# A decode step of cached attention times a gated MLP on one core: the output weight's pieces are cut at block 15 instead of 18, and one piece is spread unevenly over the DMA engines

## The chip, the core and the metric

The kernel runs on one NeuronCore of one Trainium2 chip. The metric is device time in microseconds (us), the median of repeated runs. All arithmetic is in float32. The core has a matrix engine (PE, with its weight loads listed apart as PEld), a vector engine (DVE), a scalar engine (ACT), a general engine (POOL), and a synchronising engine (SP) whose queue issues nearly all the loads. The loads are carried out by 16 DMA engines that work side by side.

## The reference, cut to what matters

```python
xn = layernorm(x)                                 # 8 tokens x 512
q = (xn @ wq).reshape(B, 1, Hq, Dh)               # 32 heads of 128
k, v = repeat(k_cache, 4), repeat(v_cache, 4)     # 8 heads of 4096 x 128 for each token
p = softmax(q @ k.T * Dh ** -0.5)
s = (p @ v).reshape(B, 1, Hq * Dh) @ wo           # wo: 4096 x 512
g = silu(gmlp(xn))                                # w_in, gelu, layernorm, w_sp, w_out
out = x + s * g
```

The caches hold 268 MB, the three weights of the attention and the MLP the rest of the 290.8 MB that are read. Every byte is used once, with eight tokens to share it.

## The kernel before, in words

**Stages.** The MLP and the query projection come first, on weights loaded into two of three large SBUF slots (`slot_b`, `slot_c`; each 128 partitions by 64 KB). Then a loop runs over 16 units, each half the tokens of one key-value head: a unit's keys arrive in `slot_a`, its values in `slot_b`. PE computes scores into the PSUM bank `sc`, DVE and ACT do the softmax, PE transposes the probabilities and multiplies them with the values, and DVE keeps the diagonal blocks of the result in `o_sb`. At the start of the next turn PE's `combine(u)` (L311 to L316) folds `o_sb` into a column of `po`, and DVE copies it to `oT`.

**The output weight.** `wo` is 4096 x 512: 32 blocks of 128 rows, block m standing in the columns m*512 to (m+1)*512 of `slot_c`, so that one block is 2 KB in each of 128 partitions, 256 KB in all. It is loaded in seven pieces that `WO_PIECES` (L29) lists by their columns: blocks 0 to 17, 18 to 21, 22 to 25, 26 and 27, 28 and 29, 30 with the first half of 31, and the second half of 31. SP issues them one after the other (L416, L417) right behind the last unit's values, each over all 128 partitions and each with a semaphore of its own, and after them `x_res`, the residual (L418). The data of one DMA engine come in the order in which SP issued them.

**The projection.** For blocks 0 to 27 (`FOLDED`), whose heads are done before the last two units end, PE multiplies `oT` with the block into one of four quarters of `sc`, the quarter being the block's number modulo 4 (L438). Before the first block of a piece `need` (L423) makes PE wait for that piece's semaphore. At block 18 (`AHEAD`) PE runs `combine` for the last unit, which waits for DVE's tokens, and DVE makes `oT_last` of it. Blocks 28 and 29 then go, in eighths of 64 columns, directly into `acc` (L448); DVE copies `sc` to `o_all` when block 27 is done; PE adds it to `acc` with a selection matrix (`pick`, L460); blocks 30 and 31 follow (L448 again), the second half of 31 waiting for the last piece. DVE multiplies by the gate and adds the residual (L469, L470), and SP stores 32 KB (L472).

What sets the order around the change is thus the program's own text: SP's queue of loads, PE's sequence of blocks and the waits that `need` puts between them.

## Time and profile before

| what | value |
|---|---|
| device time, median of 3 runs (lowest, highest) | 678.82 us (678.7, 678.97) |
| the profiled execution: its own time, its span | 678.78 us, 677.3 us |
| PE busy, share of the span | 365.7 us, 54% |
| DVE busy, share of the span | 126.6 us, 19% |
| read from HBM, mean rate over the span | 290.77 MB, 429 GB/s |

The span runs from the first to the last event that the profile shows; 1.48 us of the execution lie around it. Where the stretches of the last microseconds are listed, "PEclk" is the share of TensorE's clock that was granted, and "DMA share" the mean busy share of the 16 DMA engines; a share of 0.25 is four engines' worth. In the list of DMA issues the last number is the time from issue to landing. A wait is shown in brackets at the instruction that followed it, with the one that ended it.

### The profile page before, as it was taken

What the parts mean: (1) busy time and instruction counts of PE and PEld (TensorE: products, weight loads), DVE (VectorE), ACT (ScalarE), POOL (GpSimd) and SP (SyncE); (2) the same over time, 40 slices, a digit from 0 to 9 for tenths busy, and PEclk for the clock granted to TensorE, in tenths of its full rate; (3) what the DMA queues carried; (4) which work ended last, traced back from release to release, by engine and by line L of the source; (5) the groups of instructions that cost most, each with busy time, mean ns of one, the idle gap of its engine ahead of it and who ended that gap; (6) DMA issues with size and microseconds to landing.
All of it is one profiled execution on the core that took longest, in us unless ns stands there. A gap on an engine that the chain in (4) does not pass through costs nothing. (4 is left out here: it accounts for less than half of the span.)

```text
span 677.3 us, 6222 instructions
## 1 busy us (share of the span) xinstructions
PE 365.7 (54%) x2524; PEld 121.7 (18%) x2524; DVE 126.6 (19%) x304; ACT 17.9 (3%) x51; POOL 3.7 (1%) x16
## 2 busy tenths in 40 slices
PE   0375645445665544465564445566554546656557
PEld 0121211111221111121121112122121212112122
DVE  2420201212120211212021121212021121202012
ACT  0000000000000000000000000000000000000000
POOL 1000000000000000000000000000000000000000
PEclk9796667788776667878766677887767788776569
DMA  9999999999999999999999999999999999999997
GB/s 388 433 434 434 434 433 433 433 433 433 433 433 433 433 433 433 433 433 433 433 433 433 433 433 433 433 433 433 433 433 433 433 433 433 437 433 433 445 433 300
DMA packets 6212, 290.86 MB, mean 429 GB/s; under 512 B 952, under 2 KB 1080, under 8 KB 1472
## 3 DMA queue, kind: packets, MB, share of 16 engines
q1 hardware_dynamic: 6192, 290.79, 99.3%
q8 instruction: 3, 0.05, 0.0%
q10 hardware_dynamic: 16, 0.02, 0.0%
q14 instruction: 1, 0.01, 0.0%
HBM read 290.77 MB, written 0.03 MB: 429 GB/s over the span
## 5 line engine op out<-in xcount | busy, mean ns | idle before, releaser
L294 PE MATMUL sc<-slot,qz 128*32 128x512 f32 x1024 | 147.0, 738 | 115.4 <-PEq L286 115.4
L304 PE MATMUL o_ps<-slot,pT 128*32 128x512 f32 x1024 | 146.0, 734 | 59.0 <-PEq L286 59.0
L294 PEld LDWEIGHTS sc<-slot,qz 128*32 128x32 f32 x1024 | 40.4, 132 | 208.9 <-issue 208.9
L304 PEld LDWEIGHTS o_ps<-slot,pT 128*32 128x32 f32 x1024 | 40.2, 132 | 156.7 <-issue 156.7
L342 DVE TENSOR_REDUCE nm<-sc 128x1 f32<-128x512 f32 x16 | 11.1, 691 | 278.4 <-DVEq L352 278.4
L342 DVE TENSOR_TENSOR o_all<-o_ps,diag 128x512 f32<-128x512 f32 x32 | 22.1, 691 | 165.0 <-DVEq L352 165.0
L342 DVE TENSOR_REDUCE o_sb<-o_all 128x128 f32<-128x512 f32 x32 | 33.5, 1046 | 1.1
L314 PE MATMUL po<-fold,o_sb 128*128 128x8 f32 x68 | 13.8, 277 | 32.2 <-PEq L283 32.2
L330 PE MATMUL t<-ident,p 128*128 128x128 f32 x64 | 17.2, 424 | 19.8 <-PEq L283 19.8
L402 ACT ACTIVATE p<-sc,nm 128x512 f32<-128x512 f32 x16 | 11.0, 687 | 576.7 <-ACTq L401 576.7
L314 PEld LDWEIGHTS po<-fold,o_sb 128*128 128x128 f32 x68 | 10.9, 202 | 47.2 <-issue 47.2
L327 PE MATMUL misc<-wl,peers 128*128 128x1 f32 x32 | 6.9, 284 | 19.1 <-PEq L283 19.1
L342 DVE COPY pT<-t 128x256 f32<-128x256 f32 x32 | 12.1, 419 | 22.8 <-DVEq L352 22.8
L330 PEld LDWEIGHTS t<-ident,p 128*128 128x128 f32 x64 | 11.2, 213 | 20.7 <-issue 20.7
L323 PE MATMUL misc<-ident,nm 128*1 128x128 f32 x16 | 4.3, 269 | 17.3 <-PEq L283 17.3
L325 PE MATMUL misc<-ident,row 1*128 1x1 f32 x16 | 3.0, 189 | 15.5 <-PEq L283 15.5
L207 PE MATMUL t<-slot,xnT 128*32 128x512 f32 (+1 forms) x32 | 5.5, 785 | 9.0 <-DMA slot<-in_w_mlp 9.0
L327 PEld LDWEIGHTS misc<-wl,peers 128*128 128x128 f32 x32 | 6.0, 234 | 20.0 <-issue 20.0
L438 PE MATMUL sc<-slot,oT 128*8 128x512 f32 x56 | 7.2, 593 | 2.1 <-DMA slot<-in_wo 2.1
L342 DVE TENSOR_SCALAR p<-p,w 128x512 f32<-128x512 f32 x16 | 7.8, 486 | 0.6
L268 PE MATMUL t<-slot,xnT 128*32 128x512 f32 x64 | 7.3, 594 | 0.0
L323 PEld LDWEIGHTS misc<-ident,nm 128*1 128x1 f32 x16 | 1.3, 79 | 31.3 <-issue 31.3
(81 smaller groups left out, 75.6 us busy)
## 6 DMA issues: line engine op xcount, KB each, us to landing
slot<-in_w_mlp SPq DMA_DIRECT2D x1, 5377.0 KB, 15.5
slot<-in_wo SPq DMA_DIRECT2D x1, 4608.0 KB, 39.5
slot<-in_wo SPq DMA_DIRECT2D x2, 1024.0 KB, 42.4
slot<-in_wo SPq DMA_DIRECT2D x2, 512.0 KB, 44.6
slot<-in_wo SPq DMA_DIRECT2D x1, 384.0 KB, 45.5
slot<-in_kT SPq DMA_DIRECT2D x16, 28.2
slot<-in_v SPq DMA_DIRECT2D x16, 29.1
slot<-in_wo SPq DMA_DIRECT2D x1, 128.0 KB, 45.3
```

What stands on the lines that cost most here:

```text
L207: i = te.matmul(pz[R * g:R * (g + 1), :, :n], xnT[:, k, :], w_in[:, k, :, lo:lo + n], start=(k == 0), stop=(k == NK - 1))
L268: i = te.matmul(t[0][R * g:R * (g + 1), :], xnT[:, k, :], wq_v[:, k, lo:lo + REP * DH], start=(k == 0), stop=(k == NK - 1))
L294: i = te.matmul(sc[R * g:R * (g + 1), :], qz[:, k * R:(k + 1) * R], k_v[:, n, c, g, :], start=(k == 0), stop=(k == B - 1))
L304: i = te.matmul(of[R * j:R * (j + 1), :], pT[:, j, x, pair, e].rearrange("p x q -> p (x q)"), v_v[:, 2 * x + pair, e * (J // 2) + j], star ...
L314: i = te.matmul(po[:, bass.ds(u * N16 + pair * 2 * REP, 2 * REP)], o_sb[pair], fold.rearrange("p e r -> p (e r)"), start=True, stop=True)
L323: te.transpose(misc[:1, :P], one["nm"], ident).then_inc(for_v, 1)
L325: te.transpose(misc[:, 256:257], row.rearrange("b g n e r -> b (g n e r)"), ident[:1, :1]).then_inc(for_v, 1)
L327: te.matmul(misc[:, 320:321], peers_all, one["wl"], start=True, stop=True).then_inc(for_v, 1)
L330: i = te.transpose(t[0][:, j * P:(j + 1) * P], p[:, j, :], ident)
L342: ins = getattr(dve, name)(*args, **kw)
L402: act.activation(p.rearrange("p j s -> p (j s)"), sc, AF.Exp, bias=nm, accum_out=l).then_inc(a_turn, 1)
L438: i = te.matmul(part[R * r:R * r + B, :], oT[:, r, 2 * h + 1:2 * h + 3].rearrange("p f n -> p (f n)"), wo_v[:, m, :], start=(m < REP), sto ...
```

## The change

Two edits. First, the border of the first two pieces moves from block 18 to block 15: the first piece is 15 blocks (3840 KB), the second 7 (1792 KB). Second, the third piece (blocks 22 to 25) comes by two DMAs: its first 112 partitions in one, its last 16 in another whose source is written with an outermost dimension of 4. The 16 rows are stored on the host in such an order that they arrive where they did before. Both DMAs count on the one semaphore of the piece, so `need` waits there for 32 instead of 16.

```diff
-WO_PIECES = [(0, 18 * D), (18 * D, 22 * D), (22 * D, 26 * D), ...
+WO_PIECES = [(0, 15 * D), (15 * D, 22 * D), (22 * D, 26 * D), ...
+UNEVEN, EVEN, FEW = 2, P - 16, 4
...
     for i, (lo, hi) in enumerate(WO_PIECES):
-        load(nc.sync, slot_c[:, lo:hi], wo[:, lo:hi], f"wo{i}", *([wq_read] if i == 0 else []))
+        n = EVEN if i == UNEVEN else P
+        load(nc.sync, slot_c[:n, lo:hi], wo[:n, lo:hi], f"wo{i}", *([wq_read] if i == 0 else []))
+        if n < P:
+            load(nc.sync, slot_c[n:, lo:hi], wo[n:, lo:hi].rearrange("(b a) n -> a b n", a=FEW), f"wo{i}")
...
     def need(col):
         while seen[0] < len(WO_PIECES) and WO_PIECES[seen[0]][0] < col:
-            te.wait_ge(loaded[f"wo{seen[0]}"], 16)
+            te.wait_ge(loaded[f"wo{seen[0]}"], 32 if seen[0] == UNEVEN else 16)
             seen[0] += 1
...
+    wo = c(c(A_wo).reshape(NWO, P, D).transpose(1, 0, 2)).reshape(P, SLOT)
+    lo, hi = WO_PIECES[UNEVEN]
+    wo[EVEN:, lo:hi] = wo[EVEN:, lo:hi].reshape(FEW, (P - EVEN) // FEW, hi - lo).transpose(1, 0, 2).reshape(P - EVEN, hi - lo)
```

On PE the place is the start of the projection, behind the loop. `sc<-slot,oT` is a block of L438, `po<-fold,o_sb` the combine, and `ld_wo0` to `ld_wo3` are the pieces' semaphores. Before:

```order
L438 MATMUL sc<-slot,oT 8x512 [waits ld_wo0]
L438 MATMUL sc<-slot,oT 8x512 x17
L314 MATMUL po<-fold,o_sb 128x8 [waits tokens,ld_wo1]
L314 MATMUL po<-fold,o_sb 128x8 [waits tokens]
L438 MATMUL sc<-slot,oT 8x512 x4
L438 MATMUL sc<-slot,oT 8x512 [waits ld_wo2]
```

The same place in the changed kernel, where the line is L442:

```order
L442 MATMUL sc<-slot,oT 8x512 [waits ld_wo0]
L442 MATMUL sc<-slot,oT 8x512 x14
L442 MATMUL sc<-slot,oT 8x512 [waits ld_wo1]
L442 MATMUL sc<-slot,oT 8x512 x2
L315 MATMUL po<-fold,o_sb 128x8 [waits tokens] x2
L442 MATMUL sc<-slot,oT 8x512 x4
L442 MATMUL sc<-slot,oT 8x512 [waits ld_wo2]
```

The matrix work is the same and in the same order; only the wait for the second piece has moved, from the combine to the sixteenth block.

On SP the place is the tail of its queue of loads, with the shapes in partitions by elements. Before:

```order
L140 DMA slot<-in_wo 128x9216 [waits pe_done]
L140 DMA slot<-in_wo 128x2048 x2
L140 DMA slot<-in_wo 128x1024 x2
L140 DMA slot<-in_wo 128x768
L140 DMA slot<-in_wo 128x256
L140 DMA x_out<-in_x_res 128x64
```

In the changed kernel:

```order
L141 DMA slot<-in_wo 128x7680 [waits pe_done]
L141 DMA slot<-in_wo 128x3584
L141 DMA slot<-in_wo 112x2048
L141 DMA slot<-in_wo 16x1x2048
L141 DMA slot<-in_wo 128x1024 x2
L141 DMA slot<-in_wo 128x768
L141 DMA slot<-in_wo 128x256
L141 DMA x_out<-in_x_res 128x64
```

Seven loads of the weight have become eight, the first two cut elsewhere and the third divided by partitions; the bytes are the same.

More of the change, by code (lines that the diff above doesn't have):

```diff
@@ L28 @@
 LAST = 31 * D + D // 2
-WO_PIECES = [(0, 18 * D), (18 * D, 22 * D), (22 * D, 26 * D), (26 * D, 28 * D), (28 * D, 30 * D), (30 * D, LAST), (LAST, NWO * D)]
+WO_PIECES = [(0, 15 * D), (15 * D, 22 * D), (22 * D, 26 * D), (26 * D, 28 * D), (28 * D, 30 * D), (30 * D, LAST), (LAST, NWO * D)]
+UNEVEN, EVEN, FEW = 2, P - 16, 4
 FOLDED = NWO - REP
@@ L498 @@
         "wq": c(c(A_wq).reshape(NK, P, HKV * REP * DH).transpose(1, 0, 2)).reshape(P, SLOT),
-        "wo": c(c(A_wo).reshape(NWO, P, D).transpose(1, 0, 2)).reshape(P, SLOT),
+        "wo": wo,
         "w_mlp": np.concatenate([
```

## The prediction

> **What bounds the kernel.** I first read the page's head and the row of DMA shares, to see which engine is full.

> ```profile
> span 677.3 us, 6222 instructions
> DMA  9999999999999999999999999999999999999997
> GB/s 388 433 434 434 434 433 433 433 433 433 433 433 433 433 433 433 433 433 433 433 433 433 433 433 433 433 433 433 433 433 433 433 433 433 437 433 433 445 433 300
> ```

> The DMA engines are full in every slice but the last, at 433 GB/s, or 27.1 GB/s for each of 16. The bytes don't change, so nothing can move but the first and the last few microseconds; the edits touch only the last. Second, the chain of work that ended last, from the issue of `wo`'s first piece on.

> ```profile
> 626.13 39.50 DMA slot<-in_wo
> 665.63 0.04 issue
> 665.67 4.46 PE sc L438 x36
> 670.14 0.54 PE po L314 x4
> 670.68 2.70 PE sc L438 x20
> ...
> 673.48 0.70 DVE o_all L52
> ...
> 674.23 0.44 PE t L460 x16
> 674.67 0.52 PE t L448 x32
> ...
> 675.27 0.24 DVE gate L52
> ```

> From 665.63, when the first piece has landed, the end is set by PE alone. Six more pieces land meanwhile. When they do is read from SP's issues, seven in 3.28 us, so 0.47 apart, with the time to landing of each (the narrow windows of the DMA view, one issue each).

> ```profile
> 626.13 3.28 SPq L140 DMA_DIRECT2D slot<-in_wo  x7
> 629.45 17.55 SPq L140 DMA_DIRECT2D x_out<-in_x_res  x1
> ...
> slot<-in_wo SPq DMA_DIRECT2D x1, 1024.0 KB, 41.5
> ...
> slot<-in_wo SPq DMA_DIRECT2D x1, 1024.0 KB, 43.4
> slot<-in_wo SPq DMA_DIRECT2D x1, 512.0 KB, 44.2
> ...
> slot<-in_wo SPq DMA_DIRECT2D x1, 512.0 KB, 45.0
> slot<-in_wo SPq DMA_DIRECT2D x1, 384.0 KB, 45.5
> slot<-in_wo SPq DMA_DIRECT2D x1, 128.0 KB, 45.3
> ```

> Issue plus flight gives the landings: second piece 668.10, third 670.48, fourth 671.75, fifth 673.03, sixth 674.00, seventh 674.28. PE reaches the work that needs the sixth and seventh at about 674.46, so the data are less than half a microsecond ahead of it there. That is the floor under any gain on PE.

> **The first edit: start three blocks earlier.** Three blocks are 768 KB, which take 786,432 B / 433 GB/s = 1.82 us. The first piece then lands at 663.81 instead of 665.63. Is PE free? Its last matmuls with values:

> ```profile
> 662.56 1.05 PE L304 MATMUL o_ps<-slot,pT 128*32 128x512 f32 x8
> ```

> They end at 663.61, so PE starts at 663.85 (0.04 behind the landing, as before). How fast it goes on I take from its weight loads in order of time.

> ```profile
> 665.67 0.12 PEld L438 LDWEIGHTS sc<-slot,oT 128*8 128x8 f32 x8 [2.97 <-DMA slot<-in_wo]
> 666.11 0.11 PEld L438 LDWEIGHTS sc<-slot,oT 128*8 128x8 f32 x4 [0.32 <-issue]
> 666.54 0.11 PEld L438 LDWEIGHTS sc<-slot,oT 128*8 128x8 f32 x4 [0.32 <-issue]
> ...
> 669.11 0.10 PEld L438 LDWEIGHTS sc<-slot,oT 128*8 128x8 f32 x2 [0.33 <-issue]
> 670.07 0.52 PEld L314 LDWEIGHTS po<-fold,o_sb 128*128 128x128 f32 x4 [0.86 <-issue]
> 670.61 0.12 PEld L438 LDWEIGHTS sc<-slot,oT 128*8 128x8 f32 x8
> ```

> There is a beat of 0.43 us. Four blocks, one for each quarter of `sc`, run side by side and take two beats, 0.86 us; the 18 blocks took ten beats (665.67 to 669.97), because the last two cost as much as four. So 15 blocks are groups of 4, 4, 4 and 3: eight beats, 3.44 us, done at 667.29. Now the wait that the edit adds: block 15 needs the second piece, which lands at 668.10 as before, since the bytes up to its end are the same. PE idles 0.8 us. Queued behind that wait are blocks 15 to 17, the combine and all the rest. Blocks 15 to 17 run side by side, 668.14 to 669.00, against 669.97 before: 0.97 us won. The combine follows 0.10 later and block 18 another 0.54 later, as before: 669.64 instead of 670.61.

> From there the data come closer. Blocks 18 to 21 end at 670.50; the third piece (670.48) lets 22 to 25 run from 670.52 to 671.38; 26 and 27 wait for the fourth (671.75) and end at 672.65 instead of 673.19, 0.54 won. The copy of `sc` then ends at 673.63 and `pick` starts at 673.69. Blocks 28 and 29 lie beside the copy: they wait for the fifth piece (673.03) and issue in about half a microsecond, as before.

> ```profile
> 673.14 0.52 PEld L448 LDWEIGHTS t<-slot,oT_last 128*16 128x16 f32 x32 [0.71 <-issue]
> 674.23 0.44 PE L460 MATMUL t<-o_all,pick 128*16 128x64 f32 x16 [0.39 <-DVE o_all L52]
> 674.46 0.66 PE L448 MATMUL t<-slot,oT_last 128*16 128x64 f32 x32
> ```

> `pick` hands on after 0.23 us (674.23 to 674.46), so block 30 could start at 673.92. But the sixth piece lands at 674.00, so it starts at 674.04 instead of 674.46: **0.42 us gained**, if the landings stay. The seventh at 674.28 falls inside those 0.66 us and costs nothing. Without the sixth piece's wait the gain would be 0.54. The gate, the store and the 1.48 us around the span are the same in both.

> **The second edit: who carries the third piece.** Every DMA engine now carries 8 rows of each piece. A row of the third is 8 KB, 8,192 / 27.1 GB/s = 0.30 us. Afterwards 112 rows make 7 for each of 16, and 16 rows make 4 more for each of four engines. So twelve engines have one row less (0.30 us earlier for all that follows) and four have three more (0.91 us later). A landing is the last engine's, so it matters who is last now. The stretches at the end:

> ```profile
> 672.00:672.50 0.50, 0.50 (x10) 0.10 (x3) 0.00 (x0) 0.00 (x0) 0.00 (x0) 1.00 0.99 389
> 672.50:673.00 0.50, 0.50 (x7) 0.00 (x0) 0.00 (x0) 0.00 (x0) 0.00 (x0) 1.00 0.83 272
> 673.00:673.50 0.50, 0.50 (x25) 0.36 (x27) 0.02 (x1) 0.00 (x0) 0.00 (x0) 1.00 0.25 89
> 673.50:674.00 0.50, 0.34 (x25) 0.16 (x13) 0.50 (x1) 0.00 (x0) 0.00 (x0) 1.00 0.16 52
> 674.00:674.50 0.50, 0.28 (x19) 0.28 (x23) 0.17 (x1) 0.00 (x0) 0.00 (x0) 1.00 0.14 36
> ```

> The last two columns are the DMA share and GB/s. They do not end together: after 673.0 a share of 0.25 is four engines of 16, and then 0.16 and 0.14 two or three. Twelve are done by about 673.0, a few are up to 1.3 us behind. Two ends follow. If all the late ones are among the twelve that lose a row, the last landing comes 0.30 earlier, less what the loaded four, at 673.0 + 0.91 and a spread of some 0.3, take back: 0.05 to 0.30 earlier. If one of the late is among the loaded four, it lands 0.1 to 0.9 later. No view names the engine of a packet. Drawn blindly, the four loaded would all miss four late ones in 12·11·10·9 / (16·15·14·13) = 27% of cases, so the gain is not the safe guess; between the ends I take 0 and keep both. A shift d of the last landings moves the end by d − 0.42, down to a gain of some 0.6 where PE binds again. So the two ends are −0.6 and +0.5 us.

> The extra issue is 0.47 us of SP's queue near 628, 45 us ahead of need. Behind it the residual's issue is already held 17.55 us, to 647.0; held some microseconds longer it still joins a queue that is busy until 674, and is needed at 675.5. The clock is 1.00 in all five rows, and PE has less idle time than before, so I expect no change there.

> [...]

> **The rivals.**

> [...]

> *A late engine is among the four* (without collision): up to +0.5 us, 679.3. It belongs to the forecast's range.

> *The 16 rows don't go to four engines*: if they spread over all 16, nothing is rebalanced, d = 0, and the first edit's 0.42 remains: 678.4.

> **The numbers.** The profiled execution took 678.78, its span 677.3; the median is 678.82, 0.04 above, and I count from it. Forecast: no collision, d about 0: 678.82 − 0.42 = 678.4, own range 678.2 to 679.3; chance 0.57. Not rebalanced: 678.4, 0.07. Collision: 679.6 to 681.7, 0.36. A measurement can tell about 0.2%, 1.36 us, from no change. A gain that large is excluded by the landing floor (even landings 0.3 earlier give 0.6), 0.02 for what I don't see. Of the collision's 0.36 about two thirds exceed 1.36: slower 0.24, same 0.74. The range goes from 677.9 (a gain of 0.6 and some scatter; the three runs differ by 0.27) up to 680.8, which leaves out the upper third of the collision.

> **What would show it.** The first block's weight load at 663.85; a wait of 0.8 us for `wo` in front of block 15; block 18 at about 669.6; an unchanged second landing at 668.1. For the second edit: the seventh piece's landing beside 674.28. At 674.0 to 674.2 the late engines were relieved; at 674.4 to 675.2 the wrong ones were loaded; past 675.5 there was a collision, and the DMA share would fall below 0.9 between 668 and 671. The prediction is wrong if PE starts late in spite of the landing, or if its beat or clock changes.

## The result, and the profile after

The changed kernel takes 683.18 us (median of 6 runs, 681.72 to 683.9) against 678.85 for the kernel before on the same chip: a ratio of 1.0061, 95% interval 1.0051 to 1.0072, or 4.3 us slower. The forecast was 678.4 with a range up to 680.8. The loss lies on the side of what the prediction calls a collision, and beyond the upper end that it gave it, 681.7.

The last pieces of the changed kernel's chain of waits (start, us, what) show where the end comes from now:

```profile
626.93 47.77 DMA slot<-in_wo
674.70 0.04 issue
674.74 2.52 PE sc L442 x9
677.27 0.25 PE t L452 x5
677.52 0.56 PE sc L442 x2
...
678.17 0.70 DVE o_all L53
...
678.91 0.44 PE t L464 x16
679.36 0.52 PE t L452 x32
...
679.97 0.23 DVE gate L53
```

The chain used to enter PE at 665.67, from the first piece. Now it enters at 674.74, from the third, which lands at 674.70 instead of 670.48: 4.2 us late. Behind it blocks 22 to 27 (L442) take 3.3 us (674.74 to 678.08), part of it a wait for the fourth piece, where they took 1.9 before (671.47 to 673.36). The gate begins at 679.97 instead of 675.27, 4.70 us later in this execution, whose own time is 683.34 for a span of 682.0.

PE's weight loads in order of time, with the waits in brackets, show the first edit at work and then its loss:

```profile
664.06 0.12 PEld L442 LDWEIGHTS sc<-slot,oT 128*8 128x8 f32 x4 [0.29 <-DMA slot<-in_wo]
...
668.69 0.11 PEld L442 LDWEIGHTS sc<-slot,oT 128*8 128x8 f32 x6 [1.50 <-DMA slot<-in_wo]
669.65 0.52 PEld L315 LDWEIGHTS po<-fold,o_sb 128*128 128x128 f32 x4 [0.86 <-issue]
670.20 0.12 PEld L442 LDWEIGHTS sc<-slot,oT 128*8 128x8 f32 x8
674.74 0.12 PEld L442 LDWEIGHTS sc<-slot,oT 128*8 128x8 f32 x8 [4.43 <-DMA slot<-in_wo]
```

PE starts at 664.06, waits in front of block 15 for the second piece, which lands at 668.64, half a microsecond late already, and reaches block 18 at 670.20, still 0.4 us ahead of before. Then it stands for the third piece. What the DMA engines did meanwhile is in the stretches (the last three columns are PEclk, the DMA share and GB/s):

```profile
666.00:667.00 1.00, 1.00 (x12) 0.23 (x7) 0.76 (x1) 0.00 (x0) 0.00 (x0) 1.00 0.85 342
667.00:669.00 2.00, 1.42 (x13) 0.22 (x9) 0.00 (x0) 0.00 (x0) 0.00 (x0) 1.00 1.06 281
669.00:671.00 2.00, 2.00 (x18) 0.64 (x12) 0.29 (x2) 0.00 (x0) 0.00 (x0) 1.00 1.01 227
671.00:673.00 2.00, 0.24 (x4) 0.00 (x0) 0.00 (x0) 0.00 (x0) 0.00 (x0) 1.00 0.97 199
673.00:674.00 1.00, 0.00 (x0) 0.00 (x0) 0.00 (x0) 0.00 (x0) 0.00 (x0) 1.00 1.01 296
674.00:675.00 1.00, 0.26 (x4) 0.12 (x8) 0.00 (x0) 0.00 (x0) 0.00 (x0) 0.61 0.98 384
675.00:676.00 1.00, 1.00 (x8) 0.10 (x2) 0.00 (x0) 0.00 (x0) 0.00 (x0) 0.50 0.72 262
676.00:677.00 1.00, 1.00 (x6) 0.17 (x3) 0.00 (x0) 0.00 (x0) 0.00 (x0) 0.50 0.27 94
```

The same time in the kernel before:

```profile
666.00:668.00 2.00, 2.00 (x24) 0.55 (x20) 0.00 (x0) 0.00 (x0) 0.00 (x0) 1.00 1.02 430
668.00:670.00 2.00, 2.00 (x18) 0.30 (x8) 0.00 (x0) 0.00 (x0) 0.00 (x0) 1.00 0.98 410
670.00:672.00 2.00, 2.00 (x22) 0.95 (x22) 0.29 (x2) 0.00 (x0) 0.00 (x0) 1.00 1.01 413
```

Two things are to be seen. From 667 to 673 the engines are busy all the time, with a share of about 1.00, and move 199 to 281 GB/s instead of 410 to 430: they are as busy as before, but most packets take longer. In the trace an 8 KB packet of the third piece took 0.309 us before, every one of 128; now 0.31 to 0.94, median 0.49, and the 4 KB packets of the two pieces behind it have a median of 0.27 instead of 0.159. And at 674.2, three microseconds after PE's last matmul (671.24), its clock is granted at 0.50 for 3.4 us, just when it has to work again.

### The profile page after: what moved, and what is told of

Read it like the earlier page. It is cut to its first block, busy times and chain, and to the rows that moved or that the text cites. A ratio compares the mean times of both kernels' runs of the same rounds, so it can differ in the third digit from the quotient of the medians.

```text
span 682.0 us, 6223 instructions
## 1 busy us (share of the span) xinstructions
PE 368.3 (54%) x2524; PEld 122.7 (18%) x2524; DVE 126.7 (19%) x304; ACT 17.9 (3%) x51; POOL 3.6 (1%) x16
## 5 line engine op out<-in xcount | busy, mean ns | idle before, releaser
L305 PE MATMUL o_ps<-slot,pT 128*32 128x512 f32 x1024 | 147.8, 742 | 58.9 <-PEq L287 58.9
L442 PE MATMUL sc<-slot,oT 128*8 128x512 f32 x56 | 9.0, 681 | 4.1 <-DMA slot<-in_wo 4.1
## 6 DMA issues: line engine op xcount, KB each, us to landing
slot<-in_wo SPq DMA_DIRECT2D x2, 512.0 KB, 48.3
slot<-in_wo SPq DMA_DIRECT2D x1, 384.0 KB, 49.1
```

The costliest lines, as they stand in the source:

```text
L305: i = te.matmul(of[R * j:R * (j + 1), :], pT[:, j, x, pair, e].rearrange("p x q -> p (x q)"), v_v[:, 2 * x + pair, e * (J // 2) + j], star ...
L442: i = te.matmul(part[R * r:R * r + B, :], oT[:, r, 2 * h + 1:2 * h + 3].rearrange("p f n -> p (f n)"), wo_v[:, m, :], start=(m < REP), sto ...
```

## The experiments

All the interesting ends follow one sum, so each run is read by three numbers of its trace: the shift d of the seventh piece's landing against 674.28, the start of the gate against 675.27, and the granted clock behind the third piece. The prediction's law was that the gate moves by d − 0.42.

**One part alone.** The border only, the third piece whole:

```diff
-WO_PIECES = [(0, 18 * D), (18 * D, 22 * D), ...
+WO_PIECES = [(0, 15 * D), (15 * D, 22 * D), ...
```

> The border at block 15 alone, the third piece whole over 128 partitions as before. My step for the first edit: block 15 waits until 668.1, the sixth piece at 674.0 binds, the end is 0.42 us earlier: about 678.4 us, block 18 at 669.6, seventh landing unchanged at 674.3. Rival: the border itself costs (a wait that PE does not make good, or a lower clock): 678.8 us or more, up to the 683.2 of the whole change if it were the cause.

Measured: 678.25 us against 678.86, ratio 0.9992 (0.9983 to 1.0001). The median is 0.6 us lower in 11 runs; the interval just reaches 1. Its weight loads:

```profile
663.73 0.11 PEld L438 LDWEIGHTS sc<-slot,oT 128*8 128x8 f32 x4 [0.29 <-DMA slot<-in_wo]
...
667.95 0.11 PEld L438 LDWEIGHTS sc<-slot,oT 128*8 128x8 f32 x6 [1.11 <-DMA slot<-in_wo]
668.92 0.52 PEld L314 LDWEIGHTS po<-fold,o_sb 128*128 128x128 f32 x4 [0.86 <-issue]
669.46 0.12 PEld L438 LDWEIGHTS sc<-slot,oT 128*8 128x8 f32 x8
670.37 0.12 PEld L438 LDWEIGHTS sc<-slot,oT 128*8 128x8 f32 x8 [0.79 <-DMA slot<-in_wo]
```

Every step is within 0.2 us of where the prediction put it, and this execution's landings came 0.17 us earlier: the start (663.85 foretold), the wait in front of block 15, block 18 at 669.46 (669.64), block 22 on the heels of the third landing. The gate starts 0.58 us earlier; d is −0.17, so the law gives −0.59. The first edit is not the loss.

The uneven piece only, the border back at 18:

```diff
-WO_PIECES = [(0, 15 * D), (15 * D, 22 * D), ...
+WO_PIECES = [(0, 18 * D), (18 * D, 22 * D), ...
```

> The uneven third piece alone, border back at block 18. If the whole loss is the third piece's: its landing again near 674.7 instead of 670.5, the seventh near 678.1, DMA rate near 200 GB/s from 667 to 673, time 683.2 us or a little less (PE waits for the third piece in both, so the border is worth nothing here). If border and uneven piece only lose together: near 679 us.

Measured: 684.07 us, ratio 1.0074 (1.0059 to 1.009); third landing 674.82, seventh 678.23, 197 to 266 GB/s from 667 to 673. The whole loss is the third piece's. It is a little more than in the full change; here the clock was at 0.50 from 673.4 to 680.3, almost to the gate at 680.80.

**Which half of the uneven load.** In the trace of the change the third piece's semaphore is raised once at 628.11 and 20 times from 670.08 to 674.70, where before it was raised 16 times, from 669.16 to 670.49; that fits 16 engines for the 112 rows and four for the last 16. Here the last 16 partitions come by a plain load, by my count one row for each of 16 engines:

```diff
-load(nc.sync, slot_c[n:, lo:hi], wo[n:, lo:hi].rearrange("(b a) n -> a b n", a=FEW), f"wo{i}")
+load(nc.sync, slot_c[n:, lo:hi], wo[n:, lo:hi], f"wo{i}")
```

> The change, but the last 16 partitions of the third piece come in one plain load, one row for each of 16 engines instead of four rows for each of four. Collision among the rows of the 112-partition load: most of the loss stays, seventh landing 676.3 to 678.5, time 681 to 683.5 us, 8 KB packets still stretched. The four loaded engines as the cause: the third piece lands near 670.5 again, time about 678.5 us.

Measured: 681.71 us, ratio 1.0039 (1.0026 to 1.0052); third landing 674.05, seventh 677.50, 8 KB packets with a median of 0.48 us. Most of the loss, 2.9 us of 4.3, stays without the division by four. Then two loads of 64 partitions, both plain, with no odd count (this edit on top of that of the run before):

```diff
-UNEVEN, EVEN, FEW = 2, P - 16, 4
+UNEVEN, EVEN, FEW = 2, P // 2, 4
```

> Border at 15, the third piece as two loads of 64 partitions (0 to 63, 64 to 127), four rows for each of 16 engines in each; no odd count, no four engines. [...] If only the odd division by 7 is slow: full rate, 678.4 us.

Measured: 684.17 us, ratio 1.0072 (1.0051 to 1.0093). Its stretches:

```profile
667.00:669.00 2.00, 1.11 (x10) 0.12 (x3) 0.00 (x0) 0.00 (x0) 0.00 (x0) 1.00 1.01 188
669.00:671.00 2.00, 0.60 (x3) 0.11 (x6) 0.00 (x0) 0.00 (x0) 0.00 (x0) 0.87 0.97 211
671.00:673.00 2.00, 2.00 (x10) 0.82 (x4) 0.00 (x0) 0.00 (x0) 0.00 (x0) 0.50 1.01 221
```

Half of the 433 GB/s of the kernel before is 217, and 188 to 221 is about that, at a DMA share of 0.97 to 1.01. So it isn't the division by 7; why two halves of 64 partitions run at half the rate was not shown. The second piece lands late too, at 670.36 instead of 667.91 with the border alone. The time is far above the 678.4 expected if only the division by 7 is slow, since the third piece lands at 675.79, 5.3 us late, and since the clock is at 0.50 from 670.5 to 680.7.

**Where the collision is.** The source of the third piece in an array of its own, rows one behind the other instead of 64 KB apart:

```diff
-load(..., wo[:n, lo:hi], ...)
+load(..., wo_third[:n] if n < P else wo[:n, lo:hi], ...)
...
+"wo_third": c(wo[:, lo:hi]),
```

> The whole change, the third piece read from an array of its own with rows one behind the other instead of 64 KB apart. Collision on the way into SBUF: nothing changes, third landing near 674.7, 683.2 us. Collision while reading HBM (rows at one offset in a large pitch): the rate comes back towards 430 GB/s, third landing 670 to 672, time 678.5 to 680.5 us.

Measured: 682.84 us, ratio 1.0065 (1.0048 to 1.0082), 195 to 272 GB/s from 667 to 673. The pitch in HBM makes no clear difference (682.84 us against 683.18), which speaks for the side of SBUF.

That side can be tried by itself. Here the third piece is whole again, and behind it comes one more load of 16 rows, written with the same outermost dimension of 4, which nothing uses. Four kernels differ only in which partitions it reads for and writes (0, 32, 64 or 112):

```diff
+        if i == 2:
+            nc.sync.wait_ge(scored, U)
+            load(nc.sync, slot_a[0:16, :hi - lo], wo[0:16, lo:hi].rearrange("(b a) n -> a b n", a=4), "more")
```

> Border at 15, third piece whole over 128 partitions, and behind it one more load that nothing uses: the 16 rows of partitions 0 to 15 again, 128 KB over four engines, into partitions 0 to 15 of a free slot. [...] If it is any load over four engines that slows the rest: stretched packets, 680 us or more.

> [...] Collision by partitions: 8 KB packets stretch beyond 0.31 us, landings behind it later than with partitions 0 to 15 by 0.5 to 1.5 us, time 679.5 to 681 us. If the partitions don't matter: the same time as with 0 to 15.

> The additional 128 KB over four engines, now of and into partitions 32 to 47. [...]

> [...] If only the last partitions are special: as with 0 to 15, 678.9 us.

| partitions | time, us | ratio | 8 KB packets, us | seventh landing |
|---|---|---|---|---|
| 0 to 15 | 678.86 | 1.0001 (0.9991 to 1.0011) | all 0.309 | 674.96 |
| 32 to 47 | 678.94 | 1.0001 (0.9991 to 1.0012) | all 0.309 | 675.00 |
| 64 to 79 | 681.11 | 1.0032 (1.0018 to 1.0047) | 16 of 144 longer, up to 0.631 | 676.43 |
| 112 to 127 | 680.52 | 1.003 (1.0018 to 1.0043) | 16 of 144 longer, up to 0.636 | 676.35 |

The stretch from 670 to 671, first with partitions 32 to 47, then with 64 to 79:

```profile
670.00:671.00 1.00, 1.00 (x13) 0.12 (x8) 0.12 (x2) 0.00 (x0) 0.00 (x0) 1.00 1.02 418
```

```profile
670.00:671.00 1.00, 0.48 (x8) 0.00 (x0) 0.00 (x0) 0.00 (x0) 0.00 (x0) 1.00 0.95 197
```

The bytes and the form of the load are the same; the partitions differ, and with them the rows that are read. On 0 to 15 and 32 to 47 no packet is stretched, on 64 to 79 and 112 to 127 the whole core falls to 197 GB/s. What sets the two pairs apart the runs do not show, and no view names the engines. That the partitions written decide, and not the rows read, rests on the run with the third piece in an array of its own, where other addresses were read at about the same loss.

With partitions 0 to 15 the seventh piece lands 0.85 us later than in the run with the border alone (674.96 against 674.11; 0.68 later than in the run with the border at 16 below), and its four engines had, by my count of four rows each, 4 × 0.31 = 1.24 us more to carry. In the trace of the kernel before, twelve of the 16 counts of the seventh piece have come by 673.30, and the last comes at 674.27. So, as an estimate from these, four engines with no late one among them would have ended at 674.54 at most, about 0.3 us behind the others. That suggests that a late engine is among the four that this run loads more; it is inferred from the landings, not read off.

**The clock.** Four matmuls that nothing uses, between blocks 21 and 22 of the changed kernel:

```diff
+        if m == 22:
+            for _ in range(4):
+                te.matmul(t[0][:B], ident[:, :B], slot_c[:, :D], start=True, stop=True)
```

> The whole change with four matmuls that nothing uses between blocks 21 and 22, 3.4 us of work for PE inside its wait for the third piece. If part of the loss is the granted clock, which fell to 0.50 in that wait: the clock stays 1.00 behind 674.7, the end is set by the landings (shift 3.83 minus 0.42 = 3.4 us), 682.2 us. If the clock costs nothing: 683.2 us.

Measured: 681.84 us, ratio 1.0047 (1.003 to 1.0064), 1.3 us less than the change itself. Its stretches behind the third landing:

```profile
674.00:675.00 1.00, 1.00 (x12) 0.34 (x13) 0.00 (x0) 0.00 (x0) 0.00 (x0) 1.00 1.06 404
675.00:676.00 1.00, 0.94 (x6) 0.01 (x2) 0.00 (x0) 0.00 (x0) 0.00 (x0) 1.00 0.51 183
676.00:677.00 1.00, 0.78 (x46) 0.72 (x48) 0.69 (x1) 0.00 (x0) 0.00 (x0) 1.00 0.25 77
```

The clock stays at 1.00. Its pieces also happened to land 0.6 us earlier (seventh 677.52 against 678.11), so not all of the 1.3 is the clock's. The table below separates the two.

**Does the gain hang on block 15?** The border at 16:

> The border at block 16 instead of 15, the third piece whole. The first piece lands 0.6 us later than with 15, its 16 blocks are four whole groups and end at 667.9, still before the second landing at 668.1, so blocks 16 and 17 end at 669.0 as with 15: 678.3 us, the same. If the gain came from the early start itself it would shrink by a third: 678.45 us.

Measured: 678.31 us against 678.79, ratio 0.9993 (0.9983 to 1.0002); d is 0.00 and the gate 0.41 earlier. The landings bind there, not the start. With the border alone at 15 or 16 the kernel is about half a microsecond below the kernel before in the medians, though each interval just includes no change.

The sum over the runs, from their profiled executions:

| kernel | d | d − 0.42 | gate moved by | left over | clock behind the third piece |
|---|---|---|---|---|---|
| border 15 alone | −0.17 | −0.59 | −0.58 | 0.0 | 1.00 |
| border 16 alone | 0.00 | −0.42 | −0.41 | 0.0 | 1.00 |
| more, 0 to 15 | 0.68 | 0.26 | 0.27 | 0.0 | 1.00 |
| more, 32 to 47 | 0.72 | 0.30 | 0.31 | 0.0 | 1.00 |
| more, 112 to 127 | 2.07 | 1.65 | 1.66 | 0.0 | 1.00 |
| change, PE kept busy | 3.24 | 2.82 | 2.83 | 0.0 | 1.00 |
| the change | 3.83 | 3.41 | 4.70 | 1.3 | 0.50 |
| more, 64 to 79 | 2.15 | 1.73 | 2.81 | 1.1 | 0.50 |
| change, plain 16 rows | 3.22 | 2.80 | 3.89 | 1.1 | 0.50 |
| change, third piece from an array of its own | 3.33 | 2.91 | 4.16 | 1.2 | 0.50 |
| third piece as two halves | 4.95 | 4.53 | 6.26 | 1.7 | 0.50 |
| uneven piece alone | 3.95 | 3.53 | 5.53 | 2.0 | 0.50 |

Where the clock stays whole, the law holds to 0.01 us. Where the clock falls, 1.1 to 2.0 us come on top.

## Why the prediction was wrong, step by step

*The first edit* was right in every term, as the runs with the border alone show: the start behind the landing, the beat of 0.43 us, the wait in front of block 15, and a gain of 0.42 us bound by the landings.

*The second edit* failed at "between the ends I take 0 and keep both". The two ends, 0.3 us earlier and 0.9 us later, counted rows for each engine, at 0.30 us a row whichever partition it is for. The runs show that the partitions decide: a load of 16 rows stretches no packet on two sets of partitions and stretches 16 of 144 on two others. Why a third piece of 112 and 16 rows, or of two halves of 64, comes at 188 to 281 GB/s was not shown. In place of d = 0 came d = 3.8. That late engines might be loaded more was right (0.68 to 0.85 us with partitions 0 to 15), but small beside this.

*The collision* had the right direction, and the forecast still went the other way, at 0.57 to 0.36. Its price was too low as well: 679.6 to 681.7 rests on an estimate of mine for how much longer the third piece alone would take, a term that no run shows. What the runs showed in its place reaches beyond that piece. Packets of the third piece start at 666.3, when others of the second are still under way; three of those take up to 0.92 us instead of 0.535, and the second piece lands at 668.6 instead of 667.9 with the border alone. The 4 KB packets behind are stretched until 674.5. For six microseconds the rate is between half and two thirds of what it was.

*The clock* was expected not to change, "PE has less idle time than before". That holds for the forecast's case only. With the late third piece PE stands for 3.5 us, and 1.3 us of the profiled execution's loss are the clock's.

*What would show it* was half right: the seventh piece did land past 675.5, at 678.11, with stretched packets. But the DMA share does not fall below 0.9: it is 0.97 to 1.06 in the stretches from 667 to 673. A stretched packet counts as busy; it is the GB/s column that falls.

The sum of the 4.70 us: 3.83 later landings, 0.42 gained by the border, 1.29 lost by the clock. The extra issue cost nothing: SP's hold on the residual's load was 16.86 us instead of 17.55.

## What to carry to other kernels

Split a load by columns, not by partitions: the third piece as 112 and 16 or as 64 and 64 partitions brought the core from 410 to 430 GB/s down to 188 to 281 here, and 16 more rows did or did not, depending on their partitions. Read the DMA share together with GB/s, since stretched packets look like full use in the first, 0.97 to 1.06 here, and like half to two thirds of the speed in the second. And when a wait grows, price the clock that it may cost besides the wait itself: 1.1 to 2.0 us here.

## What the hardware showed that I had not expected

One more load of sixteen rows, 128 KB in all, on partitions 64 to 79 brought the whole core to 197 GB/s for about a microsecond, where it ran at 418 with the same load on 32 to 47. On 64 to 79 and on 112 to 127 it moved the seventh landing by 1.4 us more than on 0 to 15 or 32 to 47. That so small a load should cost all engines so much is not explained by these runs, and how the rows of a 112-partition load are given to the engines was not read off either.
